# A list-scheduled ramp replanned: mask tables on GpSimd, another order of the first loads, the state sums of unit 1 moved

## The chip, the core and the metric

The kernel runs on one core of one Trainium2 chip. The metric is the device time of one execution in microseconds (us). A core has five instruction queues that run side by side and meet only through semaphores: TensorE (PE, matrix multiplies), VectorE (DVE), ScalarE (ACT), GpSimd (POOL) and SyncE (SP), the last of which here only issues transfers. ACT and POOL issue transfers too; such an instruction stands in the engine's own order, and what is queued behind it waits until it has been issued. Each engine takes its instructions strictly in the order in which the program emits them.

## What is computed

A state-space recurrence over x (4 batches, 8 heads, 768 steps, 32 values), followed by a two-layer network with a GELU over its 3072 tokens of 256 values. Per chunk of the sequence the reference does:

```python
L = np.exp(cum[:, :, :, None] - cum[:, :, None, :]) * causal
M = np.einsum('bhin,bhjn->bhij', Cc, Bc) * L
y = M @ xc + (Cc @ state) * exp(cum)
state = decay_full * state + sum_j(Bc[j] x xc[j] * decay_from_j)
...
h = x @ w_in                  # (3072, 256) @ (256, 2048)
out = gelu_tanh(h) @ w_out    # (3072, 2048) @ (2048, 256)
```

`cum` is the running sum of log a. The kernel takes chunks of 128 steps instead of the reference's 32, which gives the same function.

## The kernel before

**Tiling.** The 3072 tokens are 24 chunks of 128, taken in 12 units of two chunks (u = 0 to 11, three units a batch). For each unit B and C (128 KB each) and x (256 KB) are loaded; B and C are scaled with decay factors (`f_mul`, line 363), transposed on TensorE (`f_T`, 384) and copied out of PSUM (`f_E`; `bt`). `f_F` (408) makes the masked copy `ce`, `f_G` (424) the 16 products that give the chunk matrices in the PSUM banks `gb`, `f_M` (434) masks their two halves into `m` (in units 0 and 1 the second half is first copied out by ACT, `f_gc`, 430). `f_D` (488) gives each chunk's addition to the state, `f_S` (516 and 518) adds it up, `f_SP` (534; `f_SP0`, 529, on ACT for chunk 0) multiplies the state by a head mask `pm`, and the session `f_Y` with `f_I` (460, 472, 447) brings `m`, x and the masked states to y in two PSUM banks, which `f_yev` copies to `xm`. Then the network: `f_s1` (551) makes 512 columns of the hidden layer out of `w_in` and `xm`, four matmuls to a step and eight steps (0 to 7) to a unit; `f_gelu` (559) is ACT's GELU; `f_s2` (568) multiplies with `w_out`; `f_oev` and `f_store` bring the result out. Here "Y0" and "Y1" are the sessions of units 0 and 1, "step i" an `f_s1` step of unit 0.

**Weights.** `w_in` and `w_out` come in quarters of 512 KB as float32 (128 partitions; runs of 2 KB for `w_in`, of 1 KB for `w_out`; B and C come in runs of 128 bytes) and are cast to bf16, by POOL (273) but for half of the last quarter of `w_out`. Steps 0 and 1 need quarter 0 of `w_in`, steps 2 and 3 quarter 1, steps 4 and 5 quarter 2, steps 6 and 7 quarter 3.

**What sets the order.** The program holds a planner, `run_order` (lines 34 to 110). Every piece of work is a node with an engine, an assumed duration, what it depends on, a priority (lower goes first) and the PSUM bank that it takes and who frees it. The planner always advances the engine that can begin first, and lets it take the ready node of lowest priority; the order in which nodes are taken is the order in which instructions are emitted. So durations and landings that the planner assumes set the order on every engine, and are nothing that the chip waits for. Where it expects TensorE to stand idle, it puts matmuls on a zero tile into the gap (`fill`, 897), as many as the gap would hold at 0.107 us for 128 columns.

**The loads.** SP issues a, C of unit 0, x of units 0 and 1 and then the order of `HEAD` (line 597); ACT issues B of unit 0, C and B of unit 1 and the four quarters of `w_in`, the last two (quarters 2 and 3) after its copy `f_rlo` (314). Eight semaphores are shared by the loads in turn, so each load waits at issue for the one eight places before it. The first load of `HEAD` behind those of ACT is held by a small POOL memset into its tile (`f_gate`, 172), which POOL reaches after the casts of x of unit 0 and of quarter 0 of `w_in`.

**Masks.** `f_par` and `f_pm` (331, 335, 337) reduce a head mask to `par` and `par4` and spread the latter to `pm`, on DVE. `f_rn`/`f_RTN` (294, 317) make the decay factors of the other batches with four matmuls, placed by the planner behind Y1.

Of the kernel before, what the change touches and what calls it, by code (L numbers as in the profile page):

```python
# [8 lines left out]
FP32 = mybir.dt.float32  # L9
BF16 = mybir.dt.bfloat16  # L10
AF = mybir.ActivationFunctionType
ALU = mybir.AluOpType
# [101 lines left out]
def kernel(  # L114
# [10 lines left out]
    nc = tc.nc  # L125

    batch, H, S, D = x.shape
    N = B.shape[-1]
# [205 lines left out]
    def f_pm():  # L334
        nc.vector.tensor_reduce(out=par4, in_=hmask.rearrange("p (w q) -> p q w", w=2),
                                op=ALU.add, axis=mybir.AxisListType.X)
        nc.vector.tensor_copy(out=pm.rearrange("p (q d) -> p q d", q=4),
                              in_=par4.rearrange("p (q o) -> p q o", o=1).to_broadcast([128, 4, D]))
# [193 lines left out]
    def f_SP(gc):  # L532
        state[("sp", gc)] = sp_new = st.tile([128, 128], BF16, name="sp_new")
        nc.vector.scalar_tensor_tensor(  # L534
            out=sp_new.rearrange("p (j d) -> p j d", j=2),
            in0=state[("s", gc)].rearrange("p (o d) -> p o d", o=1).to_broadcast([128, 2, 64]),
            scalar=pend[:, gc + 1:gc + 2], in1=pm.rearrange("p (j d) -> p j d", j=2),
            op0=ALU.mult, op1=ALU.mult)
# [77 lines left out]
    E1 = ("ACT", "ACT")  # L616
# [10 lines left out]
    def shared(n):  # L627
        n.shared = True
        return n
# [32 lines left out]
    def load_h(kind, i):  # L662
# [11 lines left out]
        n = add("DMA", DF * dur, none, deps=[lat], done=1.35 + (LATE if side is False and k > 6 else 0),  # L674
# [26 lines left out]
    cl = add("DVE", 0.55, f_clip, deps=[an], prio=-190)  # L701
    Rn = add("DVE", 0.8, f_R, deps=[cl], prio=-189)
    seln = add("DVE", 0.6, f_sel, deps=[cl, Rn], prio=-88)
    pan = add("DVE", 0.2, f_par, deps=[cl, Rn], prio=-182)
    pmn = add("DVE", 0.25, f_pm, deps=[pan], prio=-86)
    pgate = add("POOL", PG, none, prio=-300)
    pen = add("POOL", 0.6, f_pe, deps=[Rn, seln, pgate], prio=-100)
    RT0 = add("PE", 0.5, f_RT, deps=[Rn], prio=-190)
    rc0 = add("DVE", 0.2, f_rc0, deps=[RT0], prio=-180)
# [3 lines left out]
    ppn = add("PE", 0.3, f_pp, deps=[pen, RT0], prio=-100, alloc="bk")  # L713
# [7 lines left out]
    def gone(j):  # L721
        return [Yn.get(j - WB)]

    for j in range(NP):
# [7 lines left out]
        ml = {i: shared(add("DVE", 0.43, f_mul, j, i, done=0.08, prio=pj - 0.1 * i if j else -179 - i,  # L732
# [8 lines left out]
        if j == 0:  # L741
            tq = {i: add("PE", 0.14, f_T, 0, i, i + 1, deps=[ml[i]], prio=-179 - i, alloc="bk")
                  for i in (1, 0)}
# [3 lines left out]
                   add("ACT", 0.41, f_F, 0, True, (1,), "ACT", deps=[tc_, pan], prio=-178)]  # L747
# [3 lines left out]
            ec = add("ACT", 0.39, f_E, 0, 1, 2, "ACT", deps=[tq[1], *fn_], prio=-70)  # L751
# [4 lines left out]
        else:  # L756
            if j == 1:
                tq = {i: add("PE", 0.14, f_T, 1, i, i + 1, deps=[ml[i]], prio=TP - i, alloc="bk") for i in (1, 0)}
                ev = {i: add(e, 0.3 if e == "DVE" else 0.35, f_E, 1, i, i + 1, e, deps=[tq[i]], prio=PP + 2 - i)
# [16 lines left out]
            Fn[j] = [shared(add("DVE", 0.35, f_F, j, False, done=0.08, deps=[xt, *gone(j)], prio=pj + 3))] + ([ev[0]] if j == 1 else [])  # L776
# [6 lines left out]
        if u == 2:  # L783
            RTN.deps.append(Yn[1])
        if u <= MERGE:
            Gn[u] = add("PE", 0.37, f_G, u, prio=(-87, GP)[u] if u < 2 else q, deps=Fn[u] + Mn.get(u - 1, []))
# [9 lines left out]
        for r in range(2):  # L796
            gd = []
            if u < VIA and r:
                gd = [add("ACT", 1.02, f_gc, u, r, deps=[Gn[u]], prio=q if u else -80)]
            Mn[u].append(add("DVE", 0.62 if gd else 1.14, f_M, u, r, deps=[Gn[u], *gd], alloc="m", done=0.08,  # L800
                             prio=q + 1 + r if u > 1 else (-60.3, -48)[u] + 0.1 * r))
            Mn[u][-1].shared = bool(gd)
            gcn[u] = gd or gcn.get(u, [])
        for gc in nd:
# [4 lines left out]
            if gc:  # L809
                SPn[gc] = shared(add("DVE", 0.33, f_SP, gc, deps=[Sn[gc], pendn, pmn], prio=q - 0.4 if u > 1 else (-46, S1 + 0.1)[u]))  # L810
            else:
                p0n = add("ACT", 0.2, f_pp0, deps=[pmn, pendn], prio=-86)
                SPn[gc] = add("ACT", 0.8, f_SP0, deps=[Dn, p0n], prio=-61)
                frees(Dn, SPn[gc])
            frees(Dn, Sn[gc], i=gc % 2)
        full = MERGE <= u < NP - 1
        Yn[u] = add("PE", 0.42 + 0.06 * sum(gc % CPB > 0 for gc in (g0, g0 + 1)) + (0.47 if full else 0.1),
# [117 lines left out]
```

## Time and profile before

| what | value |
|---|---|
| runs shown | 115.95, 115.99 and 116.59 us, median 115.99 us |
| the profiled execution | 115.26 us |
| its span, first to last instruction | 113.6 us |
| granted TensorE clock in it | 1.00 |
| busy: PE, ACT, DVE, POOL | 106.7, 72.9, 59.1, 28.8 us |

The span is what the trace shows; the 1.66 us by which the profiled execution is longer lie around it. Rows of the timeline give start, duration, engine, line, operation, destination and source, and in brackets how long the engine sat idle before and what ended that. "ACTq" and "SPq" rows are transfers being issued. PEld is TensorE's weight load, which runs beside its matmuls; a matmul's duration holds its way through the array, so the next begins before it ends, and distances between starts tell how fast TensorE works.

### The profile page before, as it was taken

The page shows a single profiled execution, that of the slowest core. Times are in us where ns is not written, and L with a number is a line of the kernel's source. Part 1 is how long each engine was busy: PE and PEld are TensorE (multiplying, and loading weights), DVE is VectorE, ACT ScalarE, POOL GpSimd, SP SyncE. Part 2 cuts the span into 40 slices and gives each one's busy share as a digit, 9 for nine tenths or more (in the row PEclk, how much of TensorE's full clock was granted, in tenths as well). Part 3 has the DMA queues.
Part 4 walks back from the last instruction along what each step waited for, and adds up shares of the span by engine and source line. Part 5 has one row for each costly group of instructions (what it writes and reads, how often), then busy time and mean ns, then how long its engine had stood idle before and what let it go on. Part 6 is the DMA issues. An engine that isn't in the chain of part 4 may idle for free.

```text
span 113.6 us, 3920 instructions
## 1 busy us (share of the span) xinstructions
PE 106.7 (94%) x1677; PEld 87.4 (77%) x1677; DVE 59.1 (52%) x133; ACT 72.9 (64%) x160; POOL 28.8 (25%) x55
## 2 busy tenths in 40 slices
PE   5976989999999999999999999999999999999980
PEld 2453568978788887887888888879878878888860
DVE  2799793099295682913955807608819127000110
ACT  0557799932587396793783965956866847948610
POOL 6843657544440140401404112213010000000000
PEclk9999999999999999999999999999999999999999
DMA  3999999999996788938306739221131011011021
GB/s 60 259 266 369 356 326 294 205 201 215 250 178 126 98 184 52 198 92 171 99 20 141 176 47 207 75 46 46 52 88 48 9 46 55 0 46 52 0 92 49
DMA packets 47042, 15.04 MB, mean 132 GB/s; under 512 B 42320, under 2 KB 45488, under 8 KB 47024
## 3 DMA queue, kind: packets, MB, share of 16 engines
q1 hardware_dynamic: 42048, 10.19, 44.3%
q10 hardware_dynamic: 4208, 2.49, 7.3%
q0 software_dynamic: 768, 2.10, 5.0%
q8 instruction: 13, 0.21, 0.8%
q14 instruction: 5, 0.04, 0.1%
HBM read 10.58 MB, written 3.15 MB: 121 GB/s over the span
## 4 chain that ended last, share of the span: by engine, by line
PE 88%; DMA 7%; POOL 1%; DVE 1%; issue 0%; DVEq 0%; ACT 0%
PE bk L568 38%; PE bk L551 36%; DMA wf<-in_moe_w_in_dram 7%; PE gb L897 3%; PE bk L472 3%; PE gb L424 2%; PE bk L460 2%; PE bk L447 2%; PE bk L488 1%; POOL w_in_sb L273 1%; PE bk L294 1%; PE gb L294 0%; PE bk L384 0%; DVE o_sb L577 0%; DVE wz L204 0%
## 5 line engine op out<-in xcount | busy, mean ns | idle before, releaser
L559 ACT ACTIVATE gT<-bk 128x512 bf16<-128x512 f32 x96 | 50.4, 603 | 8.0 <-PE bk L551 7.8
L568 PE MATMUL bk<-w_out_sb,gT 128*128 128x256 bf16 x384 | 48.9, 273 | 0.0
L551 PE MATMUL bk<-xm,w_in_sb 128*128 128x256 bf16 x384 | 47.4, 273 | 0.5 <-POOL w_in_sb L273 0.4
L551 PEld LDWEIGHTS <-w_in_sb 128*128 128x128 bf16 x384 | 37.1, 98 | 5.7 <-POOL w_in_sb L273 1.0
L568 PEld LDWEIGHTS <-gT 128*128 128x128 bf16 x384 | 36.6, 98 | 6.2 <-issue 1.8
L434 DVE TENSOR_TENSOR m<-gb,tri 128x1024 bf16<-128x1024 f32 x22 | 26.6, 1216 | 0.6 <-PE gb L424 0.6
L582 POOL DMA_DIRECT2D out_dram<-o_sb x16 | 8.8, 552 | 46.5 <-ACT o_sb L575 44.2
L575 ACT ACTIVATE o_sb<-bk 128x256 f32<-128x256 f32 x22 | 8.5, 386 | 12.3 <-PE bk L568 6.0
L518 DVE SCALAR_TENSOR_TENSOR s_new<-s_new,pend,bk 128x64 f32<-128x64 f32 x16 | 4.4, 276 | 18.9 <-ACT xm L271 18.6
L271 ACT ACTIVATE xm<-bk 128x256 bf16<-128x256 f32 x22 | 7.3, 381 | 9.4 <-PE bk L447 6.3
L363 DVE TENSOR_TENSOR bc<-bc,fac 128x256 bf16<-128x256 f32 x24 | 9.8, 437 | 1.8 <-DMA bc<-in_C_dram 1.7
L273 POOL CAST x<-x_t 128x512 bf16<-128x512 f32 x12 | 7.5, 628 | 2.9 <-DMA x_t<-in_x_dram 2.8
L534 DVE SCALAR_TENSOR_TENSOR sp_new<-s_new,pend,pm 128x128 bf16<-128x128 f32 x19 | 8.2, 464 | 0.0
L577 DVE COPY o_sb<-bk 128x256 f32<-128x256 f32 x2 | 0.8, 424 | 14.1 <-PE bk L568 14.1
L408 DVE TENSOR_SCALAR ce<-bt,par 128x256 bf16<-128x256 bf16 x22 | 5.1, 274 | 4.3 <-ACT bt L271 4.3
L897 PE MATMUL gb<-wz 128*128 128x512 bf16 (+2 forms) x17 | 5.3, 434 | 1.3 <-DVE warm L206 1.3
L424 PE MATMUL gb<-ce,bt 32*64 32x256 bf16 x192 | 5.3, 276 | 0.4 <-ACT ce L406 0.4
L472 PE MATMUL bk<-m,x 64*32 64x128 bf16 x384 | 5.7, 218 | 0.0
L897 PEld LDWEIGHTS <-wz 128*128 128x128 bf16 x25 | 2.7, 120 | 3.8 <-issue 1.9
L516 DVE COPY s_new<-bk 128x64 f32<-128x64 f32 x3 | 0.7, 225 | 9.1 <-ACT xm L271 8.4
L273 POOL CAST w_in_sb<-wf 128x1024 bf16<-128x1024 f32 x4 | 4.3, 1082 | 2.5 <-DMA wf<-in_moe_w_in_dram 2.5
L472 PEld LDWEIGHTS <-x 64*32 64x32 bf16 x384 | 4.4, 91 | 0.0
(67 smaller groups left out, 50.9 us busy)
## 6 DMA issues: line engine op xcount, KB each, us to landing
x_t<-in_x_dram SPq DMA_DIRECT2D x12, 256.0 KB, 4.1
wf<-in_moe_w_in_dram ACTq DMA_DIRECT2D x4, 512.0 KB, 8.2
wf<-in_moe_w_out_dram SPq DMA_DIRECT2D x4, 512.0 KB, 7.0
out_dram<-o_sb POOLq DMA_DIRECT2D x16, 128.0 KB, 2.9
bc<-in_C_dram SPq DMA_DIRECT2D x11, 128.0 KB, 3.4
bc<-in_B_dram SPq DMA_DIRECT2D x10, 128.0 KB, 3.7
out_dram<-o_sb SPq DMA_DIRECT2D x8, 128.0 KB, 1.7
bc<-in_B_dram ACTq DMA_DIRECT2D x2, 128.0 KB, 4.9
```

Source lines behind the costliest of these rows:

```text
L273: nc.gpsimd.tensor_copy(out=o, in_=i)
L363: nc.vector.tensor_tensor(out=d["bc16"][:, i], in0=d["bc"][:, i].rearrange("p h (r n) -> p r h n", r=2), in1=f.rearrange("p r (h o) -> p r ...
L424: nc.tensor.matmul(out=GB[g // 2][ks, g % 2, 256 * r:256 * r + 256], lhsT=d["bt"][gs, 0, r, ks], rhs=ce[gs, :, :, ks], start=True, stop=Tr ...
L434: nc.vector.tensor_tensor(out=state[("m", u, f)].rearrange("p g r e t -> p g (r e t)"), in0=state.pop(("gc", u, f), gram[f]).rearrange("p ...
L472: nc.tensor.matmul(out=y[k][32 * q:32 * q + 32, w * Q:(w + 1) * Q], lhsT=X16[u][ks, r, 32 * h:32 * h + 32], rhs=m[w][ks, q // 2, r, q % 2, :],
L534: nc.vector.scalar_tensor_tensor(out=sp_new.rearrange("p (j d) -> p j d", j=2), in0=state[("s", gc)].rearrange("p (o d) -> p o d", o=1).to ...
L551: nc.tensor.matmul(out=hp[:, j * nt:(j + 1) * nt], lhsT=w_in_sb[:, kc, fi * 128:(fi + 1) * 128], rhs=xm[:, kc, c0 * Q:c0 * Q + nt], start= ...
L559: nc.scalar.activation(gts[g][:, i * per:(i + 1) * per, 0:nt], hps.pop((g, i)).rearrange("p (j t) -> p j t", j=per), AF.Gelu_apprx_tanh)
L568: nc.tensor.matmul(out=ops[gc], lhsT=gts[g][:, fi, tt * Q:(tt + 1) * Q], rhs=w_out_sb[:, fi, :], start=(fi == 0), stop=(fi == NF - 1), ski ...
L575: nc.scalar.activation(o_sb, ops.pop(gc), AF.Copy)
L582: q.dma_start(out=out[u * W:(u + 1) * W].rearrange("(p r) m -> r p m", r=2)[r], in_=ops.pop(gc))
L897: nc.tensor.matmul(out=bank[:, 0:128 * w], lhsT=wz[:, 0:128], rhs=wz[:, 0:128 * w], start=True, stop=True)
```

## The change

Parts that alter the order or the instructions:

- `f_pm` is made on POOL: a `tensor_tensor` of the two halves of the mask (128 x 4) in place of DVE's reduce, and the spreading copy (128 x 128). It is planned behind `f_pe` (341, 343) and so ahead of the cast of x of unit 0.
- `HEAD`: behind the gate quarter 0 of `w_out` now comes first, then B and C of unit 2, then the other quarters of `w_out`. The gate's memset goes into the tile of that quarter. POOL's order around it is as before. The priority of the matmuls `f_RTN` changes; they still stand right behind Y1.
- Half of quarter 2 of `w_out` is cast by DVE as well.
- `E1`: the B half of `bt` of unit 1 is copied out of PSUM by DVE instead of ACT.
- DVE's order in unit 1: the scaling of B directly behind the second `f_M` of unit 0; then `f_S` of chunk 1, the copy of y to `xm`, the copy of `bt`, `f_F`, `f_SP` of chunk 1, `f_S` of chunks 2 and 3, `f_SP` of chunk 2, both `f_M` of unit 1, and `f_SP` of chunk 3. Before, the `f_S` of chunk 3 stood between the two `f_M`, and the `f_SP` of chunks 2 and 3 behind both.
- PE's order: behind Y0 and the transposes of B come fills of 512 and 128 columns, step 0, `f_D` of unit 1, step 1, `f_G` of unit 1, fills of 256 and 128, steps 2 and 3, one fill of 512, steps 4 and 5, Y1, `f_RTN`, steps 6 and 7. Before: one fill of 512, the transposes, a fill of 128, `f_D`, step 0, `f_G`, steps 1 to 5, 2 fills (256 and 128), Y1, `f_RTN`, steps 6 and 7. Unit 2 is then taken up earlier: its transposes come five steps and one group of `f_s2`, its `f_G` three steps and one group sooner. From the merged sessions of unit 3 on PE's order is the same but for four `f_s2` matmuls.

The rest alters numbers that the planner assumes (durations, `LAG` for three landings, `LATE` for later ones), and switches that stay at a value without effect (`SPE = "DVE"`, `FE = 0`). The loads of x and B of unit 1 are issued by the same engines at the same places as before. The diff, cut:

```diff
-            P[j]["bc"] = ldn.tile([128, 2, H, 2 * N], FP32, name="bc")
+            if "bc" not in P[j]:
+                P[j]["bc"] = ldn.tile([128, 2, H, 2 * N], FP32, name="bc")
...
     def f_pm():
-        nc.vector.tensor_reduce(out=par4, in_=hmask.rearrange("p (w q) -> p q w", w=2),
-                                op=ALU.add, axis=mybir.AxisListType.X)
-        nc.vector.tensor_copy(out=pm.rearrange("p (q d) -> p q d", q=4),
+        nc.gpsimd.tensor_tensor(out=par4, in0=hmask[:, 0:4], in1=hmask[:, 4:8], op=ALU.add)
+        nc.gpsimd.tensor_copy(out=pm.rearrange("p (q d) -> p q d", q=4),
...
-    HEAD = [("x", 0), ("x", 1), ("b", 1), ("wi", 1), ("wi", 2), ("wi", 3), ("b", 2), ("wo", 0), ("wo", 1), ("c", 2), ("wo", 2), ("wo", 3), ("x", 2)]
+    HEAD = [("x", 0), ("x", 1), ("b", 1), ("wi", 1), ("wi", 2), ("wi", 3), ("wo", 0), ("b", 2), ("c", 2), ("wo", 1), ("wo", 2), ("wo", 3), ("x", 2)]
-    WENG = [("POOL", "POOL", "POOL", "POOL"), ("POOL", "POOL", "POOL", "POOL+DVE")]
+    WENG = [("POOL", "POOL", "POOL", "POOL"), ("POOL", "POOL", "POOL+DVE", "POOL+DVE")]
-    RP = 30
+    RP = 2000
-    GS = 0
+    GS = 1
-    LATE = 0.7
+    LATE = -0.4
+    SPE = "DVE"
+    LAG = {("x", 1): 1.0, ("b", 1): -0.6, ("wi", 3): 0.2}
-    PC = -70
-    S1 = 9.5
+    PC = -62
+    S1 = -44
+    FE = 0
-    E1 = ("ACT", "ACT")
+    E1 = ("DVE", "ACT")
...
-        n = add("DMA", DF * dur, none, deps=[lat], done=1.35 + (LATE if side is False and k > 6 else 0),
+        n = add("DMA", DF * dur, none, deps=[lat], done=1.35 + LAG.get((kind, i), LATE if not side and k > 6 else 0.0),
...
-    cl = add("DVE", 0.55, f_clip, deps=[an], prio=-190)
-    Rn = add("DVE", 0.8, f_R, deps=[cl], prio=-189)
+    cl = add("DVE", 0.42, f_clip, deps=[an], prio=-190)
+    Rn = add("DVE", 0.7, f_R, deps=[cl], prio=-189)
-    pmn = add("DVE", 0.25, f_pm, deps=[pan], prio=-86)
+    pmn = add("POOL", 0.5, f_pm, deps=[pen], prio=-99)
...
-            xd = add(f"X{u}", 0.8, none, deps=[xcn[u]]) if u else xcn[u]
+            xd = add(f"X{u}", 0.8, none, deps=[xcn[u]]) if u > 1 else xcn[u]
...
-                             prio=q + 1 + r if u > 1 else (-60.3, -48)[u] + 0.1 * r))
+                             prio=q + 1 + r if u > 1 else (-60.3, -45.5)[u] + 0.1 * r))
```

More of the change, by code (lines that the diff above doesn't have):

```diff
@@ L731 @@
         pj = PP if j == 1 else p
-        ml = {i: shared(add("DVE", 0.43, f_mul, j, i, done=0.08, prio=pj - 0.1 * i if j else -179 - i,
+        ml = {i: shared(add("DVE", 0.43, f_mul, j, i, prio=pj - 0.1 * i if j else -179 - i,
                             deps=[bl[j, i], *hold, pnn[b] if b else rlo if not i else rc1 if j else rc0, *gone(j)]))
@@ L775 @@
                         m.issued.deps.append(xt)
-            Fn[j] = [shared(add("DVE", 0.35, f_F, j, False, done=0.08, deps=[xt, *gone(j)], prio=pj + 3))] + ([ev[0]] if j == 1 else [])
+            if j == 1 and FE:
+                Fn[j] = [shared(add("DVE", 0.25, f_F, j, False, (0,), deps=[xt], prio=pj + 3)),
+                         add("ACT", 0.4, f_F, j, False, (1,), "ACT", deps=[xt], prio=pj + 2.5), ev[0]]
+            else:
+                Fn[j] = [shared(add("DVE", 0.45, f_F, j, False, done=0.08, deps=[xt, *gone(j)], prio=pj + 3))] + ([ev[0]] if j == 1 else [])
             cn = []
@@ L816 @@
         full = MERGE <= u < NP - 1
-        Yn[u] = add("PE", 0.42 + 0.06 * sum(gc % CPB > 0 for gc in (g0, g0 + 1)) + (0.47 if full else 0.1),
+        Yn[u] = add("PE", 0.42 + 0.06 * sum(gc % CPB > 0 for gc in (g0, g0 + 1)) + (0.47 if full else 0.1 if u else -0.05),
                     f_session, u, full,
```

33 lines of the change are left out of this document (17 added, 16 removed).

## The prediction, made before the changed kernel was run

> **What bounds the kernel now.** I read the page's busy times first, then the chain that ended last, then the stretch behind the ramp.
>
> ```profile
> span 113.6 us, 3920 instructions
> PE 106.7 (94%) x1677; PEld 87.4 (77%) x1677; DVE 59.1 (52%) x133; ACT 72.9 (64%) x160; POOL 28.8 (25%) x55
> PE 88%; DMA 7%; POOL 1%; DVE 1%; issue 0%; DVEq 0%; ACT 0%
> ```
>
> TensorE is busy for 94% of the span, and the chain is PE for 88% and the loading of w_in for 7%. The table by stretches shows where the rest lies:
>
> ```profile
> 16.00:110.00 94.00, 94.00 (x1510) 80.19 (x1492) 46.56 (x99) 63.66 (x138) 19.17 (x31) 1.00 0.52 112
> ```
>
> From 16 to 110 us PE is busy 94.00 of 94.00 us at full clock. No real work is lost there, and both kernels have the same real work. So only the ramp can be shortened: the question is how much earlier or later PE gets into that unbroken stretch, which begins with Y1, and whether the new order tears a hole in it. The chain in order of time says what carries the ramp:
>
> ```profile
> 5.45 8.09 DMA wf<-in_moe_w_in_dram
> 13.60 1.05 POOL w_in_sb L273
> 14.69 1.05 PE bk L551 x8
> ```
>
> Quarter 2 of w_in lands at 13.54 us, POOL casts it, and steps 4 and 5 run, with Y1 behind them. All of the ramp's last third hangs on that landing. PE's own rows:
>
> ```profile
> 9.93 0.24 PE L460 MATMUL bk<-bt,sp_new 64*32 64x128 bf16 x4 [0.67 <-ACT bt L271]
> 15.58 0.33 PE L897 MATMUL bk<-wz 128*128 128x256 bf16 x2
> 15.83 0.25 PE L460 MATMUL bk<-bt,sp_new 64*32 64x128 bf16 x8
> 17.02 2.35 PE L551 MATMUL bk<-xm,w_in_sb 128*128 128x256 bf16 x20
> ```
>
> Y0 begins at 9.93, Y1 at 15.83, step 6 at 17.02. Steps 4 and 5 (eight matmuls of 256 columns) take 15.58 - 14.69 = 0.89 us from start to start, 0.44 us a step; from Y1's start to step 6 it is 1.19 us. Between 15.58 and 15.83 PE has only fills, since Y1 waits for DVE:
>
> ```profile
> 10.31 0.42 DVE L363 TENSOR_TENSOR bc<-bc,fac 128x256 bf16<-128x256 f32 x1
> 10.65 0.42 DVE L275 CAST xm<-bk 128x256 bf16<-128x256 f32 x1
> 11.29 0.35 DVE L534 SCALAR_TENSOR_TENSOR sp_new<-s_new,pend,pm 128x128 bf16<-128x128 f32 x1
> 12.69 1.23 DVE L434 TENSOR_TENSOR m<-gb,tri 128x1024 bf16<-128x1024 f32 x1 [0.60 <-PE gb L424]
> 13.83 0.27 DVE L518 SCALAR_TENSOR_TENSOR s_new<-s_new,pend,bk 128x64 f32<-128x64 f32 x1
> 14.02 1.16 DVE L434 TENSOR_TENSOR m<-gs,tri 128x1024 bf16<-128x1024 bf16 x1
> 15.10 1.38 DVE L534 SCALAR_TENSOR_TENSOR sp_new<-s_new,pend,pm 128x128 bf16<-128x128 f32 x2
> ```
>
> The first of the two SP at 15.10 (half of 1.38, so to about 15.8) is what Y1 needs last. That is the delay that the change takes away; it is worth at most 15.83 - 15.58 = 0.25 us as long as quarter 2 lands when it does now.
>
> **The change part by part.** *Masks to POOL.* DVE loses two small operations, POOL gains two:
>
> ```profile
> 6.52 0.15 DVE L335 TENSOR_REDUCE par<-hmask 128x4 f32<-128x8 f32 x1
> 6.71 0.29 DVE L337 CAST pm<-par 128x128 bf16<-128x128 f32 x1
> 6.83 0.47 ACT L406 ACTIVATE ce<-bk,par 128x256 bf16<-128x256 bf16 x1 [1.17 <-PE bk L349]
> 7.35 0.42 PE L424 MATMUL gb<-ce,bt 32*64 32x256 bf16 x16 [0.45 <-ACT ce L406]
> 5.29 0.22 POOL L343 TENSOR_TENSOR pe<-pe,m 96x24 f32<-96x24 f32 x1
> 6.31 0.61 POOL L273 CAST x<-x_t 128x512 bf16<-128x512 f32 x1 [0.79 <-DMA x_t<-in_x_dram]
> ```
>
> The 0.44 us that DVE saves frees the copy of bt, but G of unit 0 starts at 7.35 behind ACT's ce, so on the path it is worth 0. On POOL the two have no rows. The nearest above are 0.22 us (96x24) and 0.61 us (128x512, four times as wide), so together 0.4 to 0.8 us; I take 0.45. They fit into the 0.79 us in which POOL waits for x of unit 0. Were that cover gone, D of unit 0 would come later, but Y0 is held by ACT's copy of bt until 9.93, which lies over it: cost 0.
>
> *B of unit 1 and DVE's new order.* B is issued where it was and lands 6.8 us after 3.24 us, at 10.04. DVE, which now puts its scaling straight behind M of unit 0, waits for it. From there I add the rows up: 10.1 + 0.42 (scaling) + 0.27 (S) + 0.42 (xm) = 11.2; + 0.28 for bt, which comes over from ACT, and 0.48 for the two F (rows below) = 12.0; SP 0.35, two S 0.55, SP 0.35 to 0.69 = 13.2 to 13.6; M 1.23, then M at 1.16 = 15.6 to 16.0. Y1 reads the first M at its start and the second some 0.3 us in. The S and SP no longer stand behind the M.
>
> ```profile
> 3.24 0.43 ACTq L179 DMA_DIRECT2D bc<-in_B_dram  x1
> bc<-in_B_dram ACTq DMA_DIRECT2D x1, 128.0 KB, 6.8
> 6.92 0.28 DVE L275 COPY bt<-bk 128x256 bf16<-128x256 bf16 x1
> 9.91 0.48 DVE L408 TENSOR_SCALAR ce<-bt,par 128x256 bf16<-128x256 bf16 x2 [0.20 <-ACT bt L271]
> ```
>
> *PE's new order.* Steps 0 and 1 go ahead of G: step 0 at 11.2 behind xm, D behind the cast of x, which ends at 11.43, step 1, and G at about 12.3 (ce is done at 12.0).
>
> ```profile
> 10.82 0.61 POOL L273 CAST x<-x_t 128x512 bf16<-128x512 f32 x1 [1.98 <-DMA x_t<-in_x_dram]
> ```
>
> The fills cost 0.22 us for 512 columns at the rate of the steps and lie in gaps. Steps 2 and 3 then wait, as now, for quarter 1 of w_in (its cast, below, ends at 13.22). Gain so far 0: PE only waits at another place. The end of the ramp stays with quarters 2 and 3.
>
> *w_out ahead of B of unit 2.* This is the edit that I expect to cost. SP is released by the memset in the tile behind the gate, so its next load leaves at 8.87 whichever it is, while quarters 1 to 3 of w_in are still moving on ACT's queue. Transfers per queue in 10.6 to 11.6, 12 to 13 (both queues) and 14.6 to 15.4 us:
>
> ```profile
> q10 hardware_dynamic: 211, 0.40, 104.5%
> ...
> q1 hardware_dynamic: 706, 0.12, 64.4%
> q10 hardware_dynamic: 111, 0.20, 52.5%
> ...
> q1 hardware_dynamic: 315, 0.28, 110.4%
> ```
>
> q10 is ACT's queue, q1 SP's. The engines are full in all three. Alone, a 2 KB packet of w_in costs 16 x 1.045 / 211 = 79 ns of an engine. In 12 to 13 us q1 moves almost only B, at 16 x 0.644 / 706 = 15 ns a packet; at 14.6 it is w_out, at 16 x 0.8 x 1.104 / 315 = 45 ns. B of unit 2, issued at 8.87, moved nothing before 11.6. A quarter of w_in is 256 packets, 16 to an engine. Casts begin as quarters land:
>
> ```profile
> 8.87 0.37 SPq L179 DMA_DIRECT2D bc<-in_B_dram  x1
> 12.18 1.04 POOL L273 CAST w_in_sb<-wf 128x1024 bf16<-128x1024 f32 x1 [0.75 <-DMA wf<-in_moe_w_in_dram]
> 13.60 1.04 POOL L273 CAST w_in_sb<-wf 128x1024 bf16<-128x1024 f32 x1 [0.38 <-DMA wf<-in_moe_w_in_dram]
> 15.17 1.17 POOL L273 CAST w_in_sb<-wf 128x1024 bf16<-128x1024 f32 x1 [0.53 <-DMA wf<-in_moe_w_in_dram]
> ```
>
> They come 1.42 and 1.57 us apart, 89 and 98 ns for each of 16 packets: 79 ns and one packet of B (15 ns) between every two. So the slowest engine takes the queues in turn, and a packet of w_out in B's place makes a turn 30 ns longer. If it begins to move at 12.0, as B did, about ten packets of quarter 2 and all 16 of quarter 3 meet it: quarter 2 lands 0.3 us later, quarter 3 up to 0.8 us. The Trainium skill, "DMA: Bandwidth & Descriptors", section "Queues, rings and completion order", says that each transfer engine goes round robin over the queues that have work, a packet at a time; if that holds, the sum is the one below, and if the queues kept the order of issue, it would be the one of the first rival. The distances of the casts agree with the rule.
>
> Then quarter 2's cast begins at 13.90, steps 4 and 5 at 14.99, and Y1 at 14.99 + 0.89 = 15.88, against 15.83. DVE's second M (15.6 to 16.0) just meets it. Step 6 could start at 15.88 + 1.19 = 17.07, but quarter 3 is cast from 15.97 to 17.05 and 17.10 is its start, against 17.02. So 0.25 us won and 0.33 us lost: +0.1 us. The bounds are -0.25 us (no disturbance) and +0.9 us (third rival).
>
> *Unit 2 and w_out earlier in PE's order.* C of unit 2 and quarter 1 of w_out change places, with the same bytes ahead of both together.
>
> ```profile
> 18.42 1.03 POOL L273 CAST w_out_sb<-wf 128x1024 bf16<-128x1024 f32 x1 [0.43 <-DMA wf<-in_moe_w_out_dram]
> ```
>
> Quarter 1's cast began at 18.42 and now waits for 64 more packets of 15 ns an engine: 19.4, done 20.4. Its s2 comes behind 3 + 4 steps, a group of s2 (four matmuls of 256 columns, as a step) and four transposes (512 columns), 17.1 + 7 x 0.44 + 0.44 + 0.22 = 20.8. Slack 0.4 us, taken as 0; without the cover it costs what quarter 1 is later still. DVE's added half of quarter 2 of w_out lies beside PE.
>
> *Sum.* 115.26 us for the profiled execution + 0.1 = 115.36 us. The runs shown have a median of 115.99, 0.73 above that execution; on that footing the forecast is 116.1 us, no difference that can be told.
>
> **The rivals.** *The loads don't meet* (w_out moves only behind w_in, or the slow engine is another one). Then Y1 starts at 15.58 and everything behind it 0.25 us earlier: 115.99 - 0.25 = 115.7 us. For it: w_out needs as long as B to get going. Against: B did reach the slow engine before quarter 3 was through. That the change does nothing at all of what its words say is partly so: the loads of B and x of unit 1 don't move.
>
> *A hole behind Y1.* PE reaches unit 2 five steps earlier, so quarter 1 of w_out, or B and C of unit 2 behind quarter 0, may come late. If they land 0.8 us later than I have it, the slack of 0.4 is gone and PE waits for 0.4 more on top of the 0.1: 116.5 us. For it: the engines are full all through. Against: B and C have the time of 1.3 us that steps 6 to 8 take.
>
> *The other side: w_out overtakes w_in.* If quarter 0 of w_out (32 packets of 45 ns an engine, 1.44 us, less the 20 packets or 0.3 us of B that it displaces) moves before quarter 2 is through, quarters 2 and 3 land 1.15 us later. Steps 4 and 5 start at 15.84, Y1 at 16.73, 0.90 us later, and the whole stretch with it: 116.9 us. It decides if w_out starts by about 11 us, 2.1 us behind its issue, where B took 2.7 us or more.
>
> **How the numbers follow.** The forecast (turn by turn from 12 us, 115.9 to 116.4 us) has a chance of 0.50, the undisturbed loads 0.25, the hole 0.12, the overtaking 0.10; 0.03 is for something else. The time is the likeliest's, 116.1 us. The range reaches from below the first rival to the third, 115.5 to 116.9 us; under 2 in 10 is left out. A measurement of this kernel tells about 1% (1.2 us) from no change. None of the cases passes that; some 0.1 us on top of the third, as the runs shown differ by 0.64 us, could: slower 0.10, faster 0.05, within 1% 0.85.
>
> **What would show it.** Right: the third w_in cast near 13.9 and the fourth near 16.0, no fills between step 5 and Y1 for want of DVE, Y1 at 15.8 to 16.0, G of unit 0 still at 7.35, x of unit 0 cast at 6.31, PE unbroken from 17.1. Wrong: casts at 13.6 and 15.2 (first rival), at 14.7 (third), or PE idle between 18 and 24 us (second). A Y1 that waits for an M of DVE past 16.2 would break the chain that I added up.

## The result, and the profile after

The changed kernel took 117.2 us (median of 20 runs, 115.97 to 120.96) beside 116.12 us for the kernel before (20 runs, 115.72 to 117.48). The ratio is 1.0061, 95% interval 1.0033 to 1.0088: some 0.7 us slower, under one per cent. It compares the executions in each kernel's usual, faster state alone (14 of these 20), and is therefore lower than the ratio of the two medians. Run once more on another chip (e1_again, below) it was 1.0078 (1.0042 to 1.0115). The forecast, 116.1 over 115.99, is 1.001 and lies below both intervals. The top of the range, 116.9 over 115.99, is 1.0078: the first result lies inside it, the second on its edge, and both lie above 1.0035 (116.4 us), where the forecast's own case ended.

The first profile of the changed kernel fell on an execution in which TensorE began 0.4 us late and at half speed (its numbers are in the last section); e1_again, the same kernel, began like the profile of before, so its profile is the one that I read beside it. Three lines of its page, the span, the busy times and the shares of the chain that ended last:

```profile
span 115.1 us, 3924 instructions
...
PE 107.2 (93%) x1676; PEld 87.1 (76%) x1676; DVE 58.8 (51%) x133; ACT 72.7 (63%) x159; POOL 29.9 (26%) x57
...
PE 75%; DMA 11%; SPq 7%; POOL 2%; ACTq 1%; issue 0%; DVE 0%; DVEq 0%
```

The span is 1.5 us longer, PE is busy 0.5 us longer, and the chain, 88% PE before, now runs for 11% through transfers (7% before) and for 7% through SP's queue, which was not part of it before. The PE rows from step 4 on say where PE is left waiting:

```profile
14.94 1.05 PE L551 MATMUL bk<-xm,w_in_sb 128*128 128x256 bf16 x8 [0.17 <-POOL w_in_sb L274]
15.91 0.25 PE L460 MATMUL bk<-bt,sp_new 64*32 64x128 bf16 x8
17.11 1.48 PE L551 MATMUL bk<-xm,w_in_sb 128*128 128x256 bf16 x12
20.89 0.60 PE L568 MATMUL bk<-w_out_sb,gT 128*128 128x256 bf16 x4
25.10 2.34 PE L568 MATMUL bk<-w_out_sb,gT 128*128 128x256 bf16 x20 [1.41 <-POOL w_out_sb L274]
```

Up to step 6 all is as forecast in this execution: steps 4 and 5 at 14.94, Y1 straight behind them at 15.91, step 6 at 17.11 (forecast 14.99, 15.88 and 17.10). The loss is in the last row. PE stands still for 1.41 us ahead of 25.10 and waits for POOL's cast of a quarter of w_out. The table by stretches (columns: stretch, then busy time of PE, PEld, DVE, ACT, POOL, granted clock, DMA share, GB/s) shows that this is all: 2.59 of 4.00 us busy in the second stretch, nothing lost in the others.

```profile
17.00:23.00 6.00, 6.00 (x71) 5.00 (x70) 3.19 (x6) 5.12 (x12) 2.84 (x3) 1.00 1.01 302
23.00:27.00 4.00, 2.59 (x25) 2.17 (x23) 2.84 (x4) 1.48 (x4) 1.99 (x3) 1.00 0.75 141
27.00:110.00 83.00, 83.00 (x1360) 70.78 (x1358) 40.34 (x90) 56.03 (x121) 14.48 (x25) 1.00 0.50 100
```

The hole of 1.41 us and the 0.09 us by which step 6 is later (17.11 against 17.02) make 1.50 us, and that is the difference of the two spans, 115.1 against 113.6. The medians differ by less, about 0.9 us; the profiled execution of before, 115.26 us, was one of its kernel's shorter ones.

Which quarter is late is told by POOL's casts of the changed kernel:

```profile
13.85 1.03 POOL L274 CAST w_in_sb<-wf 128x1024 bf16<-128x1024 f32 x1 [0.40 <-DMA wf<-in_moe_w_in_dram]
15.93 1.03 POOL L274 CAST w_in_sb<-wf 128x1024 bf16<-128x1024 f32 x1 [1.04 <-DMA wf<-in_moe_w_in_dram]
19.80 1.03 POOL L274 CAST w_out_sb<-wf 128x1024 bf16<-128x1024 f32 x1 [1.86 <-DMA wf<-in_moe_w_out_dram]
21.29 0.87 POOL L274 CAST w_out_sb<-wf 128x512 bf16<-128x512 f32 x1 [0.45 <-DMA wf<-in_moe_w_out_dram]
24.19 0.86 POOL L274 CAST w_out_sb<-wf 128x512 bf16<-128x512 f32 x1 [2.03 <-DMA wf<-in_moe_w_out_dram]
```

The last row is quarter 3 of w_out (DVE casts the other half at 24.16). In the kernel before it was cast at 21.94 and quarter 2 at 20.18:

```profile
20.18 1.04 POOL L273 CAST w_out_sb<-wf 128x1024 bf16<-128x1024 f32 x1 [0.72 <-DMA wf<-in_moe_w_out_dram]
21.94 0.61 POOL L273 CAST w_out_sb<-wf 128x512 bf16<-128x512 f32 x1 [0.73 <-DMA wf<-in_moe_w_out_dram]
```

Quarter 3 is 2.25 us later, with the same loads ahead of it on SP. So time of the transfer engines was lost. SP's issuing rows show where, first of the changed kernel, then of the kernel before:

```profile
8.76 0.37 SPq L268 DMA_DIRECT2D wf<-in_moe_w_out_dram  x1
9.17 0.53 SPq L180 DMA_DIRECT2D bc<-in_B_dram  x1
9.74 3.13 SPq L180 DMA_DIRECT2D bc<-in_C_dram  x1
12.91 4.37 SPq L268 DMA_DIRECT2D wf<-in_moe_w_out_dram  x3
```
```profile
9.29 2.39 SPq L267 DMA_DIRECT2D wf<-in_moe_w_out_dram  x2
11.72 2.00 SPq L179 DMA_DIRECT2D bc<-in_C_dram  x1
13.77 3.10 SPq L267 DMA_DIRECT2D wf<-in_moe_w_out_dram  x2
```

An issue can take 0.37 us. The one of C of unit 2 takes 3.13 us in the changed kernel, and of the 4.37 us of its last row the issue of quarter 1 of w_out takes 3.27. So from 9.74 to 16.18 us SP gets only these two loads out, and quarters 2 and 3 are issued at 16.22 and 16.77. Before, quarters 0 and 1 had left by 11.68, and the issues of quarters 2 and 3 began at 13.77 and 15.5. The chain that ended last in the changed kernel is made of just these pieces: the issue of C, the issue of quarter 1, the way of quarter 3 from its issue to its landing, its cast, and the matmuls behind the hole.

```profile
9.74 3.13 SPq L180
12.91 3.27 SPq L268
16.77 7.36 DMA wf<-in_moe_w_out_dram
24.19 0.87 POOL w_out_sb L274
25.10 2.34 PE bk L568 x20
```

What that did to the transfers, in the two microseconds from 14.5 to 16.5, is seen in the DMA view: first the changed kernel, then the kernel before.

```profile
DMA packets 1384, 0.26 MB, mean 130 GB/s; under 512 B 1298, under 2 KB 1375, under 8 KB 1384
```
```profile
DMA packets 1230, 0.64 MB, mean 322 GB/s; under 512 B 683, under 2 KB 1230, under 8 KB 1230
```

0.26 MB against 0.64: the changed kernel moves almost only packets of B and C (1298 of 1384 are under 512 bytes) and hardly any of w_out. At 322 GB/s the missing 0.38 MB would take 1.2 us, an estimate from these two lines.

### The profile page after: what moved, and what is told of

Same layout as the page of the kernel before. It is cut to its first block, busy times and chain, and to the rows that moved or that the text cites. A ratio compares the mean times of both kernels' runs of the same rounds, so it can differ in the third digit from the quotient of the medians.

```text
span 116.2 us, 3924 instructions
## 1 busy us (share of the span) xinstructions
PE 109.0 (94%) x1676; PEld 87.9 (76%) x1676; DVE 59.2 (51%) x133; ACT 73.0 (63%) x159; POOL 29.2 (25%) x57
## 4 chain that ended last, share of the span: by engine, by line
PE 75%; DMA 11%; SPq 8%; POOL 2%; ACTq 1%; issue 0%; DVE 0%; DVEq 0%
PE bk L568 36%; PE bk L551 30%; DMA wf<-in_moe_w_out_dram 6%; DMA wf<-in_moe_w_in_dram 5%; SPq L180 4%; SPq L268 4%; PE bk L472 2%; PE gb L424 2%; PE bk L460 2%; PE bk L447 2%; PE bk L488 1%; ACTq L180 1%; POOL w_in_sb L274 1%; POOL w_out_sb L274 1%; DVE o_sb L577 0%
## 5 line engine op out<-in xcount | busy, mean ns | idle before, releaser
L363 DVE TENSOR_TENSOR bc<-bc,fac 128x256 bf16<-128x256 f32 x24 | 10.8, 488 | 1.0 <-DMA bc<-in_B_dram 0.9
L905 PE MATMUL gb<-wz 128*128 128x512 bf16 (+2 forms) x15 | 6.0, 534 | 1.3 <-DVE warm L207 1.3
L534 DVE SCALAR_TENSOR_TENSOR sp_new<-s_new,pend,pm 128x128 bf16<-128x128 f32 x19 | 6.7, 378 | 0.0
L274 POOL CAST w_out_sb<-wf 128x1024 bf16<-128x1024 f32 (+1 forms) x4 | 3.8, 950 | 4.1 <-DMA wf<-in_moe_w_out_dram 4.1
```

What stands on the lines that cost most here:

```text
L274: nc.gpsimd.tensor_copy(out=o, in_=i)
L363: nc.vector.tensor_tensor(out=d["bc16"][:, i], in0=d["bc"][:, i].rearrange("p h (r n) -> p r h n", r=2), in1=f.rearrange("p r (h o) -> p r ...
L905: nc.tensor.matmul(out=bank[:, 0:128 * w], lhsT=wz[:, 0:128], rhs=wz[:, 0:128 * w], start=True, stop=True)
```

## The experiments

Two theories at first. *Theory A*: the hole behind Y1, which comes from the order of SP's loads (the prediction's second rival). *Theory B*, after the first profile: the clock of TensorE, which in that execution stayed low, by this theory because the first fills end before the first real matmuls begin. The second set asks which part of the change carries the loss; the third tries the prediction's other terms one by one.

**e1_again: the changed kernel, unaltered.**

> The changed kernel once more, unaltered, for a second profile. Its first profile shows two losses: TensorE at half clock up to about 9 us (128-column matmuls 0.107 us apart at 6.8 us) with G of unit 0 at 8.58 us in place of 7.35, and late loads (third w_in cast at 15.28 in place of 13.60, the second half of w_out quarter 3 at 25.24, PE idle 1.07 us before it). Theory A (the new order of loads is the cost): the casts of quarters 2 and 3 of w_in are late again, by 0.3 us or more, and time is 1.006 of before. Theory B (the first stretch of fills, three blocks of 128 columns... two blocks shorter than before, leaves TensorE cold): G of unit 0 is late again by about 1 us, time 1.006. If both losses are gone the first profile was a chance, and the time is within 0.3% of before.

1.0078 (1.0042 to 1.0115), span 115.1; its rows are above. The half-speed start was absent, the hole at quarter 3 was there again. So B is not needed for the loss.

**e2_fill: longer first fills.**

```diff
     def idle(t0, t1, j):
         n = int((t1 - max(t0, 1.26) - MARGIN) / 0.107)
+        if Gn[0].start is None and t0 < 1.3:
+            n += 4
```

> The changed kernel with four more blocks of 128 columns (0.43 us at half clock) in the first stretch of fills, so that TensorE works without a break up to the first real matmul; nothing else altered. Theory B: TensorE is at full clock from about 4.9 us, G of unit 0 at 7.3 to 7.4, and the kernel is at 0.998 of before (115.7 us). Theory A: no effect on the time, 1.006 of before; G of unit 0 may come earlier, but quarters 2 and 3 of w_in still land late and hold steps 4 to 7.

1.0059 (1.0027 to 1.0091). TensorE was at full speed early, and the hole stayed (0.96 us ahead of quarter 3, cast at 24.68). Against B.

**e3_oldloads: the changed kernel, every engine's order kept, but SP's loads in the old order.**

```diff
+    SWAP = {("wo", 0): ("b", 2), ("b", 2): ("wo", 0), ("c", 2): ("wo", 1), ("wo", 1): ("c", 2)}
...
+        kd, jd = SWAP.get((kind, i), (kind, i))
```

> The changed kernel with only the order of SP's loads put back (B of unit 2 behind the gate, then quarters 0 and 1 of w_out, then C of unit 2); all engine orders as in the changed kernel. Theory A: third and fourth w_in casts at 13.6 and 15.2, no idle PE before quarter 3 of w_out, time 0.998 of before. Theory B: G of unit 0 still late by about 1 us, time still about 1.005 of before.

1.01 (1.0058 to 1.0142): not better. The hole ahead of quarter 3 was gone. But step 6 began at 17.52 us, behind a half-speed start, PE waited 0.37 us for ACT at 18.92, and in the new order it asks for C of unit 2 earlier than the old loads bring it:

```profile
20.54 0.29 PE L384 MATMUL bk<-ident,bc 128*128 128x128 bf16 x2 [0.47 <-DVE bc L363]
```
```profile
19.66 0.82 DVE L363 TENSOR_TENSOR bc<-bc,fac 128x256 bf16<-128x256 f32 x1 [1.57 <-DMA bc<-in_C_dram]
```

**e4_both: both edits.**

> Both at once: longer first fills and the old order of loads. What is left of the change is DVE's new order, the mask tables on POOL and the earlier steps on PE. By the sum of the prediction Y1 then starts at 15.58 in place of 15.83, so 0.25 us or 0.2% less than before: 0.998. If it is at 1.006 still, the cost is in neither A nor B but in the new order of DVE and PE itself.

1.0069 (1.0035 to 1.0102). Again no hole at w_out, but Y1's second half waited 0.30 us for DVE's second M, and PE stopped once more among its steps, ahead of 18.51 (0.36 us, put down to nothing that the profile shows). In these two runs other waits took the place of the hole, so what the order of the loads costs could not be read from them. Hence the next four.

**e5_newloads: the kernel before, with only SP's load order of the change.**

```diff
+    SWAP = {("b", 2): ("wo", 0), ("wo", 0): ("b", 2), ("wo", 1): ("c", 2), ("c", 2): ("wo", 1)}
...
+        kd, jd = SWAP.get((kind, i), (kind, i))
```

> The kernel before with its own instruction orders, and of the change only the order of SP's loads behind the gate (quarter 0 of w_out, B and C of unit 2, then quarters 1 to 3). Theory that the loads alone cost: C of unit 2 holds SP for about 3.1 us instead of 2.0 us, quarters 1 to 3 of w_out leave late, quarter 2 and 3 of w_in are cast near 13.9 and 16.0 us, step 6 starts some 0.3 to 0.8 us later than 17.02 and a cast of w_out quarter 3 near 24 us; the kernel before needs that quarter about 0.9 us later than the changed one does, so some 0.3 to 1.0 us in all, 1.003 to 1.009. Rival, that only the changed PE order costs: 1.000.

1.009 (1.0053 to 1.0126), 1.0 us slower: this one edit costs as much as the whole change. SP and PE of that run:

```profile
9.87 2.66 SPq L179 DMA_DIRECT2D bc<-in_C_dram  x1
12.57 5.29 SPq L267 DMA_DIRECT2D wf<-in_moe_w_out_dram  x3
```
```profile
17.21 1.05 PE L551 MATMUL bk<-xm,w_in_sb 128*128 128x256 bf16 x8 [0.53 <-POOL w_in_sb L273]
24.29 0.60 PE L568 MATMUL bk<-w_out_sb,gT 128*128 128x256 bf16 x4 [0.74 <-POOL w_out_sb L273]
25.64 1.58 PE L568 MATMUL bk<-w_out_sb,gT 128*128 128x256 bf16 x13 [0.39 <-POOL w_out_sb L273]
```

C holds SP for 2.66 us and quarter 1 of w_out for 4.19 of the 5.29 us. PE waits for quarter 3 of w_in at step 6, for DVE's copy of y (0.55 us ahead of 18.80, behind a scaling that waited for B of unit 2), and then for quarters 2 and 3 of w_out. From 14.5 to 16.5 the engines moved 0.24 MB.

**e6_sums: the kernel before, with only the state sums of unit 1 ahead of the masks on DVE.**

```diff
-    S1 = 9.5
+    S1 = -44
...
-                             prio=q + 1 + r if u > 1 else (-60.3, -48)[u] + 0.1 * r))
+                             prio=q + 1 + r if u > 1 else (-60.3, -45.5)[u] + 0.1 * r))
```

> The kernel before with only the state sums of unit 1 ahead of the masks on DVE: both S, then M, SP of chunk 2, M, SP of chunk 3 (PE has one fill of 256 and 128 columns more, in a gap ahead of Y1). Loads, masks and the rest of PE's order are those of the kernel before. Theory of the prediction's gain: Y1 no longer waits for an SP of DVE at 15.8 and starts at 15.58 to 15.65 with quarter 2 of w_in cast at 13.60, all later work 0.2 us earlier: 0.998. Rival, that the second M now holds Y1's second half instead: 1.000 or over.

1.0009 (0.9977 to 1.0041). The forecast's gain of 0.25 us lies inside the interval, at its edge, but the trace shows no wait that could have been taken away. From step 4 to Y1 it is 1.14 us here (15.61 to 16.75), exactly as in the kernel before (14.69 to 15.83), though SP was now done 1 us ahead of Y1 (begun at 14.96, 0.74 us long). In both, PE's order holds two fills between step 5 and Y1, and the chain that ended last in the kernel before passes through them and not through DVE:

```profile
14.69 1.05 PE bk L551 x8
15.74 0.17 PE bk L897 x2
15.90 0.18 PE bk L460 x8
```

**e7_replan: the changed kernel, planned with the old load order.**

```diff
-    HEAD = [..., ("wo", 0), ("b", 2), ("c", 2), ("wo", 1), ("wo", 2), ("wo", 3), ("x", 2)]
+    HEAD = [..., ("b", 2), ("wo", 0), ("wo", 1), ("c", 2), ("wo", 2), ("wo", 3), ("x", 2)]
```

> The changed kernel with the old order of SP's loads given to the planner itself (HEAD as before), so that PE takes up C of unit 2 and the later quarters of w_out when they land in that order (casts near 17.0, 18.4, 20.2, 21.9 us; the planner has transposes of unit 2 behind step 4 of unit 1 instead of behind its step 0). Theory that loads and PE's order only have to fit each other: no hole behind step 6, Y1 near 15.6 to 15.7, 0.25 us under the kernel before, 0.998. Rival, that the rest of the new order (first fills, Y1 behind DVE's second M, stop in step 0 of unit 1 near 17.9 us) costs as in the runs with the loads swapped under the new order: 1.004 to 1.009.

0.9993 (0.9956 to 1.003). The loss is gone; no gain came in its place. All the rest of the change, with loads that fit, is worth 0 to within 0.5 us. This also speaks against B: the first fills are those of the changed kernel, and the profile shows the half-speed start, yet the median shows no loss. The profile, of an execution of 116.84 us, names one thing that cost time in it:

```profile
11.74 1.66 DVE L408 TENSOR_SCALAR ce<-bt,par 128x256 bf16<-128x256 bf16 x2
13.32 1.12 DVE L534 SCALAR_TENSOR_TENSOR sp_new<-s_new,pend,pm 128x128 bf16<-128x128 f32 x1
```
```profile
14.68 0.33 PE L905 MATMUL bk<-wz 128*128 128x256 bf16 x2 [0.81 <-DVE s_new L518]
```

DVE's F and SP came to stand beside POOL's casts and took three times as long (last section); a fill waited for S (by the planner, for the bank that S frees), and steps 2 and 3 stood behind the fill, though their quarter was cast by 13.3 us.

**e8_clate: the changed kernel, with C of unit 2 behind quarter 1 of w_out on SP, all other orders kept.**

```diff
+    SWAP = {("c", 2): ("wo", 1), ("wo", 1): ("c", 2)}
...
+        kd, jd = SWAP.get((kind, i), (kind, i))
```

> The changed kernel with every engine's order kept but for SP's: C of unit 2 and quarter 1 of w_out change places, so behind the gate come quarter 0, B of unit 2, quarter 1, C of unit 2, quarters 2 and 3. Theory that two loads of 128-byte runs in a row fill the slow transfer engine's queue and hold SP: with a quarter of w_out between them SP is held less at each, the casts of quarters 2 and 3 come 1 us or more earlier than 21.3 and 24.2 us, the hole of 1.4 us ahead of quarter 3 goes, and what is left is the wait for C of unit 2 (transposes near 18.5 us): 1.003 or less. Rival, that w_out is late only because of the bytes ahead of it: quarter 3 still cast near 24 us, 1.007.

1.0051 (1.0012 to 1.009). In the profile the mechanism came out as theory A says:

```profile
12.43 1.79 SPq L180 DMA_DIRECT2D bc<-in_C_dram  x1
14.27 3.10 SPq L268 DMA_DIRECT2D wf<-in_moe_w_out_dram  x2
```
```profile
20.06 0.61 POOL L274 CAST w_out_sb<-wf 128x512 bf16<-128x512 f32 x1 [0.56 <-DMA wf<-in_moe_w_out_dram]
22.10 0.87 POOL L274 CAST w_out_sb<-wf 128x512 bf16<-128x512 f32 x1 [1.43 <-DMA wf<-in_moe_w_out_dram]
```
```profile
DMA packets 1416, 0.63 MB, mean 313 GB/s; under 512 B 934, under 2 KB 1414, under 8 KB 1415
```

With two loads of 128-byte runs no longer in a row, 0.63 MB move from 14.5 to 16.5, quarters 2 and 3 are cast 1.2 and 2.1 us earlier than in e1_again, and PE has no hole behind step 6. Whether the time answered is not shown: the expected 1.003 or less is inside the interval, but so is the 1.0061 of the whole change. In the profiled execution the rest stands in the ramp (step 6 at 17.91), which began 0.4 us late and at half speed there (last section); whether that is so in most executions stays open.

**e9_gate: the kernel before, with the gate of SP's loads behind the cast of x of unit 1.**

```diff
-    issue[held].deps.append(add("POOL", 0.1, f_gate, *held, deps=[SPn[0] if GS else wi_n[0][-1]], prio=-98))
+    issue[held].deps.append(add("POOL", 0.1, f_gate, *held, deps=[SPn[0] if GS else wi_n[0][-1], xcn[1]], prio=-98))
```

> The kernel before with the gate of SP's loads behind the cast of x of unit 1 on POOL (end at 11.43 us) instead of ahead of it (8.8 us); nothing else moves. It tests the forecast's turn-by-turn term in the other direction: B of unit 2 no longer takes a 15 ns turn between two packets of quarters 2 and 3 of w_in, so these are cast up to 0.25 and 0.5 us earlier than 13.60 and 15.17 us, 1.3 us apart as 16 packets of 79 ns, while the casts of w_out come 0.5 to 1 us later than 16.95, 18.42, 20.18 and 21.94 us. Y1 stays held by DVE's SP at 15.8, so 1.000; slower, 1.003 to 1.008, if w_out now comes too late for PE behind 20 us. Rival, that the loads do not share the slow engine's time: casts of w_in unchanged.

1.001 (0.9969 to 1.0051).

```profile
11.76 1.04 POOL L273 CAST w_in_sb<-wf 128x1024 bf16<-128x1024 f32 x1 [0.41 <-DMA wf<-in_moe_w_in_dram]
13.12 1.04 POOL L273 CAST w_in_sb<-wf 128x1024 bf16<-128x1024 f32 x1 [0.32 <-DMA wf<-in_moe_w_in_dram]
14.42 1.03 POOL L273 CAST w_in_sb<-wf 128x1024 bf16<-128x1024 f32 x1 [0.26 <-DMA wf<-in_moe_w_in_dram]
```

The last two distances are 1.36 and 1.30 us instead of 1.42 and 1.57: 81 ns for each of 16 packets in the last, as against the 79 ns that a packet takes alone. So the turn between two packets is all but gone. That the slowest engine had no packet of SP's yet is inferred: SP's packets move from 12.2 us on, and the trace does not tell on which engine. The rule of the Trainium skill, "DMA: Bandwidth & Descriptors", section "Queues, rings and completion order", that an engine goes round robin over the queues that have work, agrees with this as it did with the distances of before. The earlier quarters were of no use to this execution: PE, which began late, ran without a break from step 1 at 13.32 to the fills behind step 5, and DVE's SP, begun at 15.92, held up the first matmuls of Y1 (0.52 us from 16.04 instead of 0.25). The time did not move.

**e10_gatesums: that gate and the sums together.**

> The gate of the run above and the state sums of unit 1 ahead of the masks together, on the kernel before: with earlier quarters 2 and 3 of w_in and no SP to wait for, Y1 could begin at 15.4 to 15.6 instead of 15.83 us and step 6 at 16.5 to 16.8 instead of 17.02: 0.996 to 0.998 if w_out is still in time. Rival, that w_out comes late: over 1.000.

1.0004 (0.9969 to 1.004): no gain. In its profile x of unit 1 landed late (cast at 12.15, so the gate opened at 12.70), quarter 3 of w_out was cast at 24.46, and PE waited 0.79 us for it at 25.38: the rival's side. It is also the nearest to a version better than both kernels that the runs suggested, and it is none.

**e11_cold: the kernel before, with 12 blocks of 128 columns fewer among the first fills.**

```diff
+        if Gn[0].start is None and t0 < 1.3:
+            n -= 12
```

> The kernel before with 12 blocks of 128 columns fewer among the first fills, so that TensorE is idle for some 1.3 us ahead of its first real matmuls at 4.49 us. Theory that the clock state of the first 9 us is what separates executions of one kernel: TensorE stays at half clock to 8 us or later in every execution (fills of 512 columns 0.40 instead of 0.21 us apart behind 5 us), G of unit 0 at 7.8 to 8.6 and Y0 at 10.4 to 11.4 us, and the time is 0.5 to 1.0 us longer, 1.004 to 1.009, without short executions near 115.5 us. Rival, that quarters 2 and 3 of w_in hide it: 1.000.

1.0021 (0.9981 to 1.0061). The fills behind the first matmuls show the low speed (three in 1.24 us, in the kernel before 0.70), and Y0 came 1.36 us later at 11.29, and Y1's last inputs 0.94 us later than 15.83. Yet the median moved by 0.24 us (-0.2 to +0.7), which can't be told from nothing. What it was compared with is a mixture: of the six profiles with the first fills of the kernel before, three begin slowly, too (e6_sums, e10_gatesums, e12_masks). At the middle of the interval the effect is a third of the loss, e1_again, e2_fill and e5_newloads have the loss in profiles without the slow start, and e7_replan has the slow start in its profile and no loss in its median. Theory B falls as the main cause.

```profile
5.31 1.24 PE L899 MATMUL gb<-wz 128*128 128x512 bf16 x3
11.29 0.24 PE L460 MATMUL bk<-bt,sp_new 64*32 64x128 bf16 x4
16.77 0.25 PE L460 MATMUL bk<-bt,sp_new 64*32 64x128 bf16 x7 [0.25 <-DVE sp_new L534]
```

**e12_masks: the kernel before, with only the mask tables on POOL.**

```diff
-    pmn = add("DVE", 0.25, f_pm, deps=[pan], prio=-86)
+    pmn = add("POOL", 0.5, f_pm, deps=[pen], prio=-99)
```

(with the two instructions of `f_pm` on `nc.gpsimd` as in the change)

> The kernel before with only the mask tables made on POOL (two small operations behind the one of line 343, ahead of the cast of x of unit 0) instead of DVE. The forecast says 0: POOL needs 0.4 to 0.8 us in a wait of 0.79 us, G of unit 0 stays at 7.35 us behind ACT's copy: 1.000. Rival, that the cast of x of unit 0 or of quarter 0 of w_in is pushed back by POOL: 1.002 or more.

0.9966 (0.9923 to 1.001): nothing, or a gain too small to tell. The two operations took 0.19 and 0.29 us, and POOL then still waited 1.42 us for x of unit 0, which landed late in that execution.

## Why the prediction came out as it did, step by step

- *Where it counts.* Only the ramp can change, and a hole can be torn into the stretch behind it: right, to the table of stretches.
- *Masks to POOL, 0.* Right (e12_masks). In e1_again they took 0.44 and 0.36 us, the upper bound, and the cast of x of unit 0 began straight behind them at 6.36 against 6.31. G of unit 0 came at 7.21, not at 7.35, behind ACT's ce, which began 0.15 us sooner; why is not settled.
- *The gain, at most 0.25 us.* Its reason was misread. The two SP at 15.10 did not take half of 1.38 us each: by the trace one took 0.34 and the other 1.12, so the first was done at 15.44, 0.39 us ahead of Y1. What lay between step 5 and Y1 were two fills that PE's order held there: 0.25 us from the first fill to Y1 in the kernel before, and 0.25 or 0.26 in e5_newloads, e6_sums and e12_masks as well, with SP done 0.4 to 1.0 us ahead of Y1. The changed order has no fills there, and the way from step 4 to Y1 is 0.97 us in e1_again instead of 1.14. So 0.17 us were to be had, by leaving out the fills; that this moved the time is neither shown nor excluded. (DVE's SP does hold Y1 in other executions, in e9_gate and e11_cold.)
- *DVE's chain to the second M, 15.6 to 16.0.* It ended at 15.4 in e1_again, early enough; in e4_both and e7_replan it came late and held Y1's second half for 0.30 and 0.29 us, as the last sentence of the prediction had feared.
- *w_out's turns between the packets of w_in.* Right in kind and size. The distances between casts tell it best: from quarter 2 to quarter 3 it was 2.08 us in e1_again, 1.99 in the first profile of the changed kernel and 2.02 in e2_fill and e8_clate, where 2.07 was forecast; in six profiles with B of unit 2 first it was 1.51 to 1.61. e9_gate shows the reverse. In e1_again the times themselves agree as well: casts at 13.85 and 15.93 (forecast 13.90 and 15.97), Y1 at 15.91 (15.88), step 6 at 17.11 (17.10). That is partly luck, since in the first profile and in e2_fill quarter 1 landed later and Y1 began at 17.35 and 16.85. In e5_newloads quarter 3 of w_in was cast at 16.12, 3.03 us behind quarter 2, a microsecond more than the forecast's term; why it was so much there is not settled.
- *Unit 2 and w_out earlier in PE's order: "Slack 0.4 us, taken as 0".* This is the step that failed. Quarter 1 itself was cast at 19.80 instead of 19.4 and just used up the slack: its group began at 20.89 with no wait. But the sum went by quarter 1 alone. It counted "the same bytes ahead of both together", and left out that SP issues in order and that an issue can be held. C of unit 2, now the second of two loads of 128-byte runs in a row, held SP for 3.13 us and quarter 1 behind it for 3.27; quarters 2 and 3 were cast 1.1 and 2.25 us later, and PE waited 1.41 us for the last. PE's new order did not make this worse: ahead of quarter 3 it has the same work in both kernels, and reached it 6.4 us behind step 6 before (23.38) and 6.6 in e1_again (23.69). (The expectation of e5_newloads put 0.9 us between the two orders there.) The price of this step was +0.6 to +0.8 us in the median instead of 0.
- *The rivals.* The second, a hole behind Y1, is what happened, at quarter 3 instead of quarter 1 and with 0.7 to 0.9 us in place of 0.5; it had a chance of 0.12. It came on top of the forecast's terms and not instead of them. The first, undisturbed loads, is excluded by the distance from quarter 2 to quarter 3; the third too, which needs 2.57 us from the cast of quarter 1 to that of quarter 2 (12.18 to 14.75), where the five profiles with w_out first have 1.36 to 1.76. That the first result lies inside the range is therefore luck in part: the upper end was set by the third rival, which did not happen.

What is shown and what isn't: it is shown that the order of the loads carries the loss (e5_newloads has all of it, e7_replan none), and that transfers ran dry while SP was held in two issues (0.26 and 0.24 MB in e1_again and e5_newloads, 0.64 and 0.63 in the kernel before and e8_clate). That C's place does this is shown for the transfers by the one profile of e8_clate, and not for the time. That SP is held because the queue of one slow transfer engine is full is only argued. What speaks for it is that the issue of quarter 1 ends at 16.18 us in e1_again, 0.25 us behind the start of the last w_in cast, and that in e5_newloads, from 16.8 to 17.1 us, only 32 packets move, all under 512 bytes, at a DMA share of 0.09: one or two of the 16 engines still work off B and C while the others are idle. Old loads under the new PE order (e3_oldloads 1.01, e4_both 1.0069) are as slow as new loads under the old one (e5_newloads, 1.009), and so is the change itself, new loads under the order planned for them. Only old loads with an order planned for them were as fast as the kernel before (e7_replan).

## What to carry to other kernels

When loads change places, walk the issuing queue as you walk an engine: which issue is long, what stands behind it, and when the last of those is needed, not only the first. Two loads cut into many small packets are better not issued in a row ahead of large ones: here the queue was then held for 6.4 us in two issues while the transfer engines ran empty, and a load of longer runs between them kept the engines full. An order that a planner made for one set of landings is not to be judged with another. And work that ends shortly before another piece begins has not held it for that reason: ask the chain, or a run that moves one of the two.

## What the runs showed of the hardware that was not expected

**Some of DVE's instructions wait for POOL's to end.** The two F take 0.48 us with POOL idle (the row in the prediction) and 1.66 us in e7_replan, where they begin 0.02 us behind a cast of POOL and the next cast follows; an SP takes 0.34 alone (e1_again, at 15.35) and 1.12 there. They end at 13.40 and 14.44 us, 0.1 and 0.15 us behind the end of a cast. (M keeps its length: 1.21 us in e1_again, from 13.52, beside a cast from 13.85.) POOL's rows of that run:

```profile
11.72 0.61 POOL L274 CAST x<-x_t 128x512 bf16<-128x512 f32 x1 [3.07 <-DMA x_t<-in_x_dram]
12.27 2.02 POOL L274 CAST w_in_sb<-wf 128x1024 bf16<-128x1024 f32 x2
```

The Trainium skill, "SBUF — State Buffer", section "SBUF: two separate sides", says that GpSimd and some instructions of VectorE share a pair of ports by an exclusive lock held for a whole instruction; the lengths agree. A like difference stands at the very start. In the kernel before the clip of a, which everything waits for, took 0.29 us; in e8_clate a landed 0.08 us later, and the clip took 0.57, in both beside POOL's making of the masks:

```profile
3.23 0.29 DVE L285 TENSOR_SCALAR ac<-a_t 96x256 f32<-96x256 f32 x1 [1.63 <-DMA a_t<-in_a_dram]
```
```profile
3.31 0.57 DVE L286 TENSOR_SCALAR ac<-a_t 96x256 f32<-96x256 f32 x1 [1.71 <-DMA a_t<-in_a_dram]
```

The first matmuls then began at 4.88 instead of 4.49. That POOL's work holds the clip is not shown: in e6_sums a clip begun at 3.30 took 0.29. But here the ramp started 0.4 us later behind a landing less than 0.1 us later, and four of the fourteen profiled executions, the first of the changed kernel among them, began at 4.88.

**TensorE's speed at the start changes from execution to execution.** In the first profile of the changed kernel the three fills behind the first matmuls took 1.24 us, in e1_again 0.70, with the same instructions; two transposes began 0.21 us before the next pair (6.76 to 6.97), in e1_again 0.12 (5.92 to 6.04). Eight of the fourteen profiles begin with the 1.24 us, among them kernels with either set of first fills. The granted clock that the profile shows is 1.00 all the same (in the first profile from 5 to 9 us), so the half speed is read from the distances alone. The Trainium skill, "TensorE: Matmul & The Clock Gate", section "Part 1: The HAM clock gate", says that the gate looks at windows that run freely and that warming up differs between runs; this agrees. What it costs is bounded only by the ratio of e11_cold, against a mixture.

**Landings spread by more than the change is worth.** x of unit 1, whose load nothing here changed, was cast at 10.36 us in e4_both and at 12.22 us in the first profile of the changed kernel.
